# Convolution and SwiGLU block: unit 1 moved from TensorE to a channel-major convolution on the other engines, unit 2 moved to TensorE, with a shorter start

## The chip, the cores and the metric

The kernel runs on one core of a Trainium2 chip. The metric is the device time of one execution in microseconds (us). Times are medians over some executions with their range.

In this program matrix products are on TensorE (PE); VectorE (DVE), ScalarE (ACT) and GpSimd (POOL) do elementwise work. GpSimd also starts the loads that cast float32 to float16, and SyncE (SP) starts nearly all other transfers, one after the other.

## The reference

A depthwise causal convolution with seven softmax weights a head is followed by a SwiGLU block:

```python
w = softmax(weight)                        # (8 heads, 7 taps)
x_pad = pad 6 zeros ahead of x             # x: (8, 4096, 192)
out[b, s, h, g] = sum_k w[h, k] * x_pad[b, s + k, h, g]     # 24 channels a head
g = out @ w_gate;  v = out @ w_val         # (192, 1536) each
result = (g * sigmoid(g) * v) @ w_out      # (1536, 192), 32768 tokens in all
```

## The kernel before

The 32,768 tokens are 64 blocks of 512, and four blocks are a unit. A block is 12 steps. A step multiplies a block with 128 columns of the gate and of the value weights (three matmul pairs each), ACT makes the SiLU, DVE the product, and the down projection follows some steps later. So step n belongs to block n // 12 and unit n // 48.

There are three ways to convolve. Unit 0 has a special early path. Units 1 and 3 are done on TensorE by banded matmuls, in two halves of 32 matmuls placed between steps. All others ("pooled") are done with channels on partitions:

```python
POOLED = (2, *range(4, NU))                 # NU = 16 units

def cast_x(u):      # POOL: one casting load of a unit's input, DRAM to DRAM scratch, ~770 KB
    xs[u] = dpool.tile([rows, D], fp16, tag="xs", name="xs")
    seq(nc.gpsimd.dma_start(out=..., in_=...))          # [cut]

def turn_x(u, i, at):   # SyncE: scratch to SBUF, transposed; needs the whole cast
    seq(nc.sync.dma_start_transpose(out=t, in_=rows[:, at : at + P]))

def place(u, i):        # SyncE: four copies that build the two shared channel tiles of a block
    t0, t1, t2 = xc[b]
    y = y2[u, i // 2][Q * (i % 2) : Q * (i % 2) + Q, :]
    for dst, src in (
        (t1[0:Q, 0:TB], t0[Q:P, 0:TB]), (t1[Q:P, 0:TB], y),
        (t2[0:Q, 0:TB], y),             (t2[Q:P, 0:TB], t0[0:Q, 0:TB]),
    ):
        seq(nc.sync.dma_start(out=dst, in_=src))
```

A pooled unit has six jobs: four of kind "block" (128 of the 192 channels of a block) and two of kind "pair" (the remaining 64 channels of two blocks). In a job ACT makes two or three of the seven taps, DVE two, which it adds itself, and POOL the others and the remaining sums. A block can be placed when its own job and its pair's job are done. The program decides at which step each transfer enters SyncE's order:

```python
def planned(v):                             # steps at which the transfers of unit v are queued
    ...
    if v == 2:   cast, jobs = 21, 55;  times = (36, 36, 36, 38, 39, 39, 41, 41, 43, 43)
    elif v == 3: cast, jobs = 60, 56;  times = range(66, 86, 2)         # [not used: 3 is on TensorE]
    else:        cast, jobs = s0 - 115, s0 - 89;  times = range(s0 - 105, s0 - 85, 2)   # s0 = 48 v

done = max(finished[job] for job in need)   # program step at which POOL's part is queued
if n < max(done + (12 if u == 2 else 18), ustep * u + NCH * i - 16):
    break
place(u, i)
```

## Time and profile before

| | before |
|---|---|
| median of 3 runs | 779.17 us (777.87 to 779.5) |
| span of the profiled run | 776.0 us |
| TensorE busy | 767.9 us, 99% |
| clock granted to TensorE | full from 3.67 us to the last matmuls |
| first gate matmul | 8.43 us |
| plain block of 12 steps | 11.73 us |
| gate matmuls waiting for copies `pxc<-pxc`, `pxc<-y` | none |

`xs<-in_x_dram` is the casting load of a pooled unit, `x<-xs` a transpose out of it (or, as a plain copy `x<-x` of 66 KB, the join of two halves), `pxc<-pxc` and `pxc<-y` the copies of `place`, `x<-x` in a pair of 480 KB the `dup_x` of a TensorE unit, `scr<-tm` the writes of a TensorE unit's result to scratch. A gate matmul `gate<-pxc` needs what POOL wrote itself and, from the second of its three pairs on, what `place` copied.

### The profile page before, as it was taken

What the parts mean: (1) busy time and instruction counts of PE and PEld (TensorE: products, weight loads), DVE (VectorE), ACT (ScalarE), POOL (GpSimd) and SP (SyncE); (2) the same over time, 40 slices, a digit from 0 to 9 for tenths busy, and PEclk for the clock granted to TensorE, in tenths of its full rate; (3) what the DMA queues carried; (4) which work ended last, traced back from release to release, by engine and by line L of the source; (5) the groups of instructions that cost most, each with busy time, mean ns of one, the idle gap of its engine ahead of it and who ended that gap; (6) DMA issues with size and microseconds to landing.
All of it is one profiled execution on the core that took longest, in us unless ns stands there. A gap on an engine that the chain in (4) does not pass through costs nothing.

```text
span 776.0 us, 27834 instructions
## 1 busy us (share of the span) xinstructions
PE 767.9 (99%) x11179; PEld 599.6 (77%) x11179; DVE 687.4 (89%) x1034; ACT 607.6 (78%) x1067; POOL 597.8 (77%) x551
## 2 busy tenths in 40 slices
PE   8999999999999999999999999999999999999997
PEld 5666666668888888888888888888888888887876
DVE  7687998999999999999999999999999999997775
ACT  6576887888878878878888888888888788776664
POOL 9100697799999999999999999999999999992000
PEclk9999999999999999999999999999999999999999
DMA  9949854754534536255353443535445352221211
GB/s 136 186 117 125 170 127 102 166 102 102 114 95 104 103 94 124 65 118 118 84 112 86 103 111 77 115 88 116 93 105 115 77 122 70 70 66 38 70 57 42
DMA packets 143651, 79.31 MB, mean 102 GB/s; under 512 B 89146, under 2 KB 143042, under 8 KB 143042
## 3 DMA queue, kind: packets, MB, share of 16 engines
q1 hardware_dynamic: 130690, 61.58, 34.8%
q0 software_dynamic: 12832, 15.96, 13.5%
q8 instruction: 87, 1.43, 0.8%
q14 instruction: 42, 0.34, 0.1%
HBM read 31.92 MB, written 37.83 MB: 90 GB/s over the span
## 4 chain that ended last, share of the span: by engine, by line
PE 97%; POOL 1%; DMA 1%; DVE 1%; issue 0%; ACT 0%; DVEq 0%; POOLq 0%
PE val L777 41%; PE acc L803 33%; PE gate L777 22%; DMA xe<-in_x_dram 1%; POOL w L168 0%; DVE h L788 0%; POOL xe L98 0%; PE cv L476 0%; PE acc L824 0%; PE cv L387 0%; PE turn L445 0%; ACT sig L786 0%; DVE o_sb L862 0%; ACT o_sb L970 0%; POOL jn L192 0%
## 5 line engine op out<-in xcount | busy, mean ns | idle before, releaser
L786 ACT ACTIVATE sig<-gate 128x512 f16<-128x512 f32 x768 | 448.9, 599 | 154.6 <-PE gate L777 105.3
L788 DVE TENSOR_TENSOR h<-sig,val 128x512 f16<-128x512 f16 x768 | 495.2, 683 | 79.4 <-PE gate L777 45.9
L777 PEld LDWEIGHTS <-w 64*128 64x128 f16 x4608 | 338.9, 110 | 135.2 <-issue 1.9
L777 PE MATMUL gate<-pxc,w 64*128 64x512 f16 x1872 | 438.7, 376 | 0.0
L777 PE MATMUL val<-pxc,w 64*128 64x512 f16 x1872 | 437.6, 376 | 0.5
L803 PE MATMUL acc<-wo,h 64*128 64x192 f16 x6096 | 329.7, 243 | 0.8 <-issue 0.7
L803 PEld LDWEIGHTS <-h 64*128 64x128 f16 x6096 | 300.6, 94 | 28.2 <-ACT sig L786 2.1
L632 POOL TENSOR_TENSOR total<-total,part 128x512 f32<-128x512 f32 x130 | 173.0, 1330 | 45.6 <-DVE total L657 21.8
L657 DVE SCALAR_TENSOR_TENSOR total<-x,both_taps,total 128x512 f32<-128x512 f16 x156 | 166.3, 1066 | 0.0
L647 POOL TENSOR_SCALAR piece<-x,both_taps 128x512 f32<-128x512 f16 x182 | 154.4, 848 | 0.0
L632 POOL TENSOR_TENSOR total<-total,piece 128x512 f32<-128x512 f32 x104 | 141.6, 1362 | 8.7
L777 PE MATMUL gate<-xc,w 64*128 64x512 f16 x432 | 102.1, 377 | 0.0
L777 PE MATMUL val<-xc,w 64*128 64x512 f16 x432 | 101.9, 376 | 0.1
L682 ACT ACTIVATE part<-x,both_taps 128x512 f32<-128x512 f16 x130 | 93.3, 718 | 0.0
L632 POOL TENSOR_TENSOR pxc<-total,piece 128x512 f16<-128x512 f32 x52 | 70.3, 1353 | 4.3
L682 ACT ACTIVATE total<-x,both_taps 128x512 f32<-128x512 f16 x78 | 55.7, 714 | 0.0
L632 POOL TENSOR_TENSOR y<-total,piece 128x512 f16<-128x512 f32 x26 | 33.1, 1273 | 2.2
L862 DVE COPY o_sb<-acc 128x384 f32<-128x384 f32 x63 | 34.5, 547 | 0.0
L861 ACT COPY o_sb<-acc 128x384 f32<-128x384 f32 x63 | 29.6, 471 | 0.1
L98 POOL DMA_DIRECT2D x<-in_x_dram x6 | 5.1, 870 | 24.4 <-ACT sig L786 24.4
L504 POOL COPY tm<-tm 128x1280 f16<-128x1280 f16 x2 | 2.5, 1249 | 19.5 <-DVE tm L493 19.5
L590 POOL DMA_DIRECT2D xs<-in_x_dram x13 | 7.2, 555 | 0.0
(67 smaller groups left out, 74.1 us busy)
## 6 DMA issues: line engine op xcount, KB each, us to landing
out_dram<-o_sb SPq DMA_DIRECT2D x63, 384.0 KB
pxc<-pxc SPq DMA_DIRECT2D x104, 64.0 KB
pxc<-y SPq DMA_DIRECT2D x104, 64.0 KB
xs<-in_x_dram POOLq DMA_DIRECT2D x7, 768.0 KB, 6.7
xs<-in_x_dram POOLq DMA_DIRECT2D x6, 774.0 KB, 6.7
x<-in_x_dram POOLq DMA_DIRECT2D x6, 480.0 KB, 9.4
scr<-tm SPq DMA_DIRECT2D x14, 130.0 KB
x<-x SPq DMA_DIRECT2D x26, 66.0 KB
```

What stands on the lines that cost most here:

```text
L98: nc.gpsimd.dma_start(out=t[p0 + i0 : p0 + i1, w0 - at : w1 - at, :], in_=bass.AP(tensor=x_flat.tensor, offset=(t0 + size * w0 - pad + i0) ...
L590: nc.gpsimd.dma_start(out=flat[skip * D : rows * D].rearrange("(a n) -> a n", n=n), in_=bass.AP(tensor=x_flat.tensor, offset=(u * UT - XP ...
L632: nc.gpsimd.tensor_tensor(job["dst"] if k == K - 1 else total, total, part, op=ALU.add)
L647: nc.gpsimd.tensor_scalar(part, shifted(k), scalar1=job["tap"][:, k : k + 1], scalar2=1.0, op0=ALU.mult, op1=ALU.mult,)
L657: nc.vector.scalar_tensor_tensor(job["total"], shifted(k), job["tap"][:, k : k + 1], job["total"], op0=ALU.mult, op1=ALU.add,)
L682: nc.scalar.activation(part, shifted(k), AF.Copy, scale=job["tap"][:, k : k + 1])
L777: nc.tensor.matmul(o, w16[m][p0 : p0 + Q, k, e::E], xc[b][k][p0 : p0 + Q, 0:TB], start=(k == 0), stop=(k == SL - 1),)
L786: silu[n] = seq(nc.scalar.activation(sg, g, AF.Silu)).ins
L788: seq(nc.vector.tensor_tensor(hj, sg, v, op=ALU.mult))
L803: nc.tensor.matmul(acc[b][bank][:, s, :], hj[p0 : p0 + Q, ts(2 * bank + s, P)], wo16[p0 : p0 + Q, j, :], start=(not second and j == 0 and ...
L861: seq(nc.scalar.copy(o_sb[:, 0:2, :], acc[b][0]))
L862: seq(nc.vector.tensor_copy(o_sb[:, 2:4, :], acc[b][1]))
```

## The change

The intent is to take one of two convolved units off TensorE, the busiest engine. Unit 1 becomes pooled, which fills the time in which POOL, DVE and ACT have room; unit 2 takes the TensorE path in its place, and unit 3 is pooled like the later ones. The start is trimmed as well: fewer fillers before the tap matmuls, the band built by halves of the heads, the value weights in one transfer a third.

```diff
-    POOLED = (2, *range(4, NU))
+    POOLED = (1, *range(3, NU))
 [load_w: value weights in one transfer a third, not two, so a step reads its weight slices in rotated order; iota behind it]
-    x16_tile(1)                      # unit 1's four loads for TensorE
-    for r in range(2):
-        for low in (0, 32):
-            load_x(1, r, low=low)
 [tap matmuls and band by halves of the heads, each half in one PSUM bank]
-        if v == 2:
-            cast, jobs = 21, 55
-            times = (36, 36, 36, 38, 39, 39, 41, 41, 43, 43)
-        elif v == 3:
-            cast, jobs = 60, 56
-            times = range(66, 86, 2)
+        if v == 1:
+            jobs = 19
+            times = (13, 13, 14, 15, 16, 24, 25, 26, 28, 30)
         else:
-            cast, jobs = s0 - 115, s0 - 89
+            jobs = s0 - 89
             times = range(s0 - 105, s0 - 85, 2)
-        plan.setdefault(cast, []).append(lambda: cast_x(v))
+            plan.setdefault(s0 - 115, []).append(lambda: cast_x(v))
 [taps also at steps 20, 23 and 26]
-            if n < max(done + (12 if u == 2 else 18), ustep * u + NCH * i - 16):
+            if n < max(done + (9 if u == 1 else 18), ustep * u + NCH * i - 16):
-    keep_warm(8)
+    keep_warm(6)
+    keep_warm(1, P)
     spread_taps()
-    keep_warm(4, 2 * P)
+    keep_warm(5, 2 * P)
 [...]
+    cast_x(1)
-        at = (25, 31) if u == 0 else (10, 22)     # steps of the convolution halves
+        at = (10, 22)
```

More of the change, by code (lines that the diff above doesn't have):

```diff
@@ L127, in x16_tile, with load_x @@
         x16[u] = cpool.tile([P, 4 * NG, D], fp16, tag="x16", name="x16")
-    def load_x(u, r, after=None, low=0):
-        t, t0, w0, p0 = x16[u], u * UT, 4 * NG * r, Q * r + low
+    def load_x(u, r, after=None):
+        t, t0, w0, p0 = x16[u], u * UT, 4 * NG * r, Q * r
         w1 = w0 + 4 * NG
@@ L161, in load_w @@
         f0, f1 = WF * m, WF * m + WF
-        for half, src, i0, i1, s0 in (
-            (0, moe_w_gate, 0, SL, 0),
-            (1, moe_w_val, 0, SL - 1, 1),
-            (1, moe_w_val, SL - 1, SL, 0),
-        ):
+        for half, src in enumerate((moe_w_gate, moe_w_val)):
             seq(
                 nc.gpsimd.dma_start(
-                    out=w16[m][Q * half : Q * half + Q, i0:i1, :],
-                    in_=src[Q * s0 : Q * (s0 + i1 - i0), f0:f1].rearrange(
-                        "(s q) f -> q s f", q=Q
-                    ),
+                    out=w16[m][Q * half : Q * half + Q],
+                    in_=src[:, f0:f1].rearrange("(s q) f -> q s f", q=Q),
                 )
@@ L195 @@
     xe_load(0)
+    load_w(0)
     cid = small("cid", [P, P], i32)
     seq(nc.gpsimd.iota(cid, pattern=[[1, P]], base=0, channel_multiplier=0))
-    load_w(0)
     load_w(1)
@@ L328, in make_wide @@
         ]
-        for n in range(4):
-            c0 = 16 * 2 * H * (n % 2)
-            seq(
-                nc.tensor.matmul(
-                    banks[n // 2][:, c0 : c0 + 16 * 2 * H],
-                    shift[:, n].rearrange("p r i -> p (r i)"),
-                    spread.rearrange("p j a h -> p (j a h)"),
-                    start=(n % 2 == 0),
-                    stop=True,
-                    skip_group_check=True,
-                )
-            )
-        seq(nc.vector.tensor_copy(pf, pid))
-        for h0 in (0, 4):
+        half = H // 2
+        for hh in range(2):
+            for n in range(4):
+                c0 = 16 * H * n
+                seq(
+                    nc.tensor.matmul(
+                        banks[hh][:, c0 : c0 + 16 * H],
+                        shift[:, n].rearrange("p r i -> p (r i)"),
+                        spread[:, :, :, half * hh : half * hh + half].rearrange(
+                            "p j a h -> p (j a) h"
+                        ),
+                        start=(n == 0),
+                        stop=True,
+                        skip_group_check=True,
+                    )
+                )
+        for hh in range(2):
             for n in range(2):
@@ L345, in make_wide @@
                     (nc.scalar.copy, nc.vector.tensor_copy)[n](
-                        wide[:, :, h0 : h0 + 4, 32 * n : 32 * n + 32],
-                        banks[n].rearrange("p (j a h) -> p a h j", a=2, h=H)[
-                            :, :, h0 : h0 + 4, :
-                        ],
+                        wide[:, :, half * hh : half * hh + half, 32 * n : 32 * n + 32],
+                        banks[hh][:, 32 * H * n : 32 * H * n + 32 * H].rearrange(
+                            "p (j a h) -> p a h j", a=2, h=half
+                        ),
                     )
                 )
+        seq(nc.vector.tensor_copy(pf, pid))
         seq(
@@ L746, in pooled_work @@
         step_now[0] = n
-        if not busy and j != 4:
+        if not busy and (j in (1, 7, 10) or n in (20, 23, 26)):
             ready = dve_steps[0][0] if dve_steps else None
             ahead = act_steps[0][0] if act_steps else n_jobs[0]
-            if j in (1, 7, 10) and ready is not None:
+            if ready is not None:
                 dve_steps.pop(0)[1]()
-            if j in (1, 7, 10) and act_steps and (ready is None or ahead < ready + 3):
+            if act_steps and (ready is None or ahead < ready + 3):
                 act_steps.pop(0)[1]()
@@ L778, in gate_val @@
                         o,
-                        w16[m][p0 : p0 + Q, k, e::E],
+                        w16[m][p0 : p0 + Q, (k + half) % SL, e::E],
                         xc[b][k][p0 : p0 + Q, 0:TB],
@@ L932 @@
             efetch(3)
-        if n == 34:
+        if n == 10:
             make_picks()
-        if n == 37:
+        if n == 13:
             make_channel_taps()
@@ L946 @@
                     conv_out(u + 1, m)
-            lo = 32 if u == 0 else 28
-            if ls in range(lo, lo + 12, 3):
-                fetch(UB * (u + 1) + (ls - lo) // 3)
+            if ls in range(28, 40, 3):
+                fetch(UB * (u + 1) + (ls - 28) // 3)
         if u + 2 < NU and not pooled(u + 2):
```

## The prediction

> **What bounds the kernel now.** I read the page's busy shares first, then the slices, the chain that ended last, the windows by block, and last the early chain in order of time.
>
> ```profile
> PE 767.9 (99%) x11179; PEld 599.6 (77%) x11179; DVE 687.4 (89%) x1034; ACT 607.6 (78%) x1067; POOL 597.8 (77%) x551
> ...
> POOL 9100697799999999999999999999999999992000
> PEclk9999999999999999999999999999999999999999
> ...
> PE 97%; POOL 1%; DMA 1%; DVE 1%; issue 0%; ACT 0%; DVEq 0%; POOLq 0%
> ```
>
> TensorE is busy 99% of the span at full clock, and 97% of the chain is TensorE. POOL is nearly full from slice 6 (about 100 us) to slice 36 (about 700 us), but idle in slices 3 and 4 (about 40 to 75 us): there is room for POOL work early and none in the middle.
>
> The program makes 64 blocks of 12 steps. A block's start is that of its first gate matmul in the trace: 8.43, 20.34, 37.59, 50.85, 62.89 us and so on. Windows on those starts (columns: length; busy us and count of PE, PEld, DVE, ACT, POOL; clock; DMA share; GB/s):
>
> ```profile
> 8.43:20.34 11.91, 11.62 (x177) 6.99 (x177) 8.57 (x15) 8.07 (x15) 11.01 (x20) 1.00 1.29 180
> 20.34:37.59 17.25, 16.36 (x350) 11.56 (x347) 11.34 (x20) 9.78 (x19) 2.04 (x5) 1.00 1.43 199
> 37.59:50.85 13.26, 13.26 (x237) 9.01 (x233) 11.04 (x19) 9.58 (x17) 1.25 (x1) 1.00 0.41 99
> 62.89:74.62 11.73, 11.73 (x170) 8.00 (x168) 8.38 (x13) 8.15 (x14) 1.71 (x2) 1.00 1.21 134
> 86.35:98.08 11.73, 11.73 (x170) 8.00 (x168) 11.26 (x16) 9.65 (x17) 11.32 (x11) 1.00 0.88 207
> 109.81:122.18 12.37, 12.37 (x202) 8.29 (x200) 11.89 (x18) 10.07 (x18) 11.82 (x11) 1.00 0.49 105
> ```
>
> A plain block takes 11.73 us, also with DVE at 11.26 and POOL at 11.32 of it. The block at 109.81 has 32 more matmuls, half a unit's convolution on TensorE, and takes 12.37: **0.64 us a half**. So whatever is on TensorE counts at full price, and what the other engines do costs nothing while they keep up. 64 x 11.73 = 750.7 of the 776.0 us; the other 25 us are the start, extra TensorE work in the first blocks, the tail, and a few bubbles.
>
> The early chain (columns: start us, us, what):
>
> ```profile
> 1.42 2.17 POOL xe L98 x3
> ...
> 3.84 3.43 POOL w L168 x6
> ...
> 7.87 6.29 DMA xe<-in_x_dram
> 14.21 0.72 PE cv L387 x59
> ...
> 35.96 0.72 issue
> 39.60 0.59 PE cv L476 x32
> ```
>
> The first 14 us are ruled by POOL issuing loads and by the second input load, which lands at 14.16 us. At 35.96 TensorE loses 0.72 us to "issue": it waits for no semaphore.
>
> [...] the chain here shows steps of 0.21 us per gate and val pair, [...] the eight 512-wide fillers run 0.43 us apart until 4.2 us and the 256-wide ones after that 0.11 us apart, [...] here every cast load has a POOL issue of 0.55 to 0.87 us. [...]
>
> **The change, part by part.**
>
> 1. *One unit fewer on TensorE.* Of 16 units, before convolves 1 and 3 on TensorE, after only 2 (unit 0 is early work in both).
>
> ```profile
> L476 PE MATMUL cv<-x,band 64*32 64x240 f16 x128 | 2.6, 266 | 0.0
> L493 DVE CAST tm<-cv 128x480 f16<-128x480 f32 x8 | 4.9, 650 | 0.1
> L493 ACT CAST tm<-cv 128x480 f16<-128x480 f32 x8 | 4.1, 562 | 2.1 <-PE cv L476 2.1
> ```
>
> 128 matmuls become 64, in two halves of 32: 2 x 0.64 = **-1.28 us**, straight off the path. The compiled order confirms it: 60 matmuls fewer (-64, +4 for the halved taps). The four DVE and four ACT evictions of the unit (2.6 and 2.2 us) go too, beside the path.
>
> 2. *Unit 1 goes to ACT, DVE and POOL*: 6 jobs more, 84 for 78.
>
> ```profile
> L632 POOL TENSOR_TENSOR total<-total,part 128x512 f32<-128x512 f32 x130 | 173.0, 1330 | 45.6 <-DVE total L657 21.8 <-ACT sig L786 19.6
> L657 DVE SCALAR_TENSOR_TENSOR total<-x,both_taps,total 128x512 f32<-128x512 f16 x156 | 166.3, 1066 | 0.0
> L647 POOL TENSOR_SCALAR piece<-x,both_taps 128x512 f32<-128x512 f16 x182 | 154.4, 848 | 0.0
> L682 ACT ACTIVATE part<-x,both_taps 128x512 f32<-128x512 f16 x130 | 93.3, 718 | 0.0
> ```
>
> POOL's five convolution groups sum to 572 us over 78 jobs, 7.3 us each, so +44 us on POOL; DVE +12 x 1.07 = 13 us; ACT +16 x 0.72 = 11 us. All of it lies between steps 20 and 75, where POOL had 2.04 and 1.25 us of work in two blocks. Off the path: **0**, if the tiles arrive in time. I followed the program's rule for placing them: unit 1's blocks are copied into place at steps 40, 46, 64 and 76 and needed at 48, 60, 72 and 84; the slack is 8 steps at the least, where unit 2 before had 11. In time: the first two jobs have their last DVE part at step 31, about 45 us, POOL then ends near 53, the copies land near 57, and step 48 comes near 61. For the last block POOL ends near 91, SyncE is then busy with unit 2's nine writes to scratch (they took 6 us for unit 1 before), so the copies may land at 94 to 96 and step 84 comes at 96.5. That margin is about 1 us, and I charge **+0.2 us** for it. From unit 4 on jobs run only 3 steps later than before and are still placed 16 steps ahead: no change.
>
> 3. *Start.* Two fewer fillers and taps by half: the tap matmuls come about 0.4 us earlier and the first copies need one bank only. But the first input load lands at 5.79 and the band is used at 6.08, so at most 0.3 us of this is real; then the first gate weights (landed 8.21) and value weights (8.84 and 9.13) bind. The value weights now are one transfer of 192 KB, which I put at 9.0: the first step gains nothing. One POOL issue fewer per third (0.57 us each) and the iota behind them: DMA engines are by then 1.29 full in the mean, so landing, not issue, rules; I put the second input load 0.3 us earlier. **-0.3 us**, where early work waits for it at step 6.
>
> 4. *Traffic.* Four loads of 480 KB, issued from 16.9 us and landing at 24 to 33 us, are gone; one cast to scratch (landed at 36.4 for unit 2) takes their place and should land near 24. Eight transposes through SyncE (1.25 us each) follow; the first convolution on ACT comes at step 20, near 33 us, so 5 us later than its tile. The 0.72 us of "issue" fell just as the old burst drained. It has an even chance to vanish: **-0.35 us**.
>
> Sum: -1.28 - 0.3 - 0.35 + 0.2 = -1.7; 779.17 - 1.7 = **777.4 us**.
>
> **The rivals.** *A late unit 1.* [...] if the cast lands after 33 us the SiLU behind the first tap waits and TensorE with it; the same if a copy into place is late. For it: margins of 8 steps, and a landing of 36.4 us for the comparable cast before. Against: that one was issued at 21.98 us behind four large loads; now it goes out near 17.5. Cost if it happens: 1 to 4 us, so 778 to 781. *POOL becomes the bound*, since it already is full from 100 to 700 us. Against: the new work lies before that, and placement keeps 16 steps of slack; else 14 units x 44 = 616 us must fit in about 680. I give it little; it would show as several us at unit starts. *The start pays more*: if all of the earlier issue reaches the path and the "issue" gap goes, the gain is 1.28 + 1.0 + 0.7 = 3 us, 776.2. *The conv removed is hidden anyway*: TensorE's extra 0.64 us in the block at 109.81 is measured, so no.
>
> **Range and chances.** The before runs spread over 1.6 us, and bubbles of 0.03 to 0.32 us in the middle blocks sum to some 1.8 us that can come or go. With the rivals: 775.5 to 779.2. 2% is 15.6 us: nothing above comes near it, in either direction. Within 2%: 0.98; 0.01 each side.
>
> **What would show it.** Step 1: 64 convolution matmuls, and one pair of 12.37 us blocks left, moved to units' steps 58 and 70. Step 2: blocks 4 to 7 at 11.73 us apart from those 0.64 us, with POOL full from about 37 us; wrong if a gate matmul at steps 48, 72 or 84 waits for a DMA into the placed tiles, or if ACT's first tap waits for a transpose. Step 3: the first gate matmul within 0.3 us of 8.43 and early work after step 6 before 14.0. Step 4: no "issue" piece of over 0.5 us in the first 45 us. The whole is wrong if the time falls under 775.5 or rises over 779.2.

## More of the kernel before

A unit for TensorE needs its input four times shifted in SBUF; half of this is loaded and the other half comes from `dup_x`, two plain SyncE copies of 480 KB, each partition's row in one piece. (Unit 1 of this kernel loads all four itself, so here only unit 3 has a `dup_x`.)

The page's line of the gate matmuls that read placed tiles (busy us, mean ns, then the idle time before them):

```profile
L777 PE MATMUL gate<-pxc,w 64*128 64x512 f16 x1872 | 438.7, 376 | 0.0
```

## The result, and the profile after

| | before | changed |
|---|---|---|
| median, same session | 778.98 us (777.87 to 779.5, 4 runs) | 786.09 us (783.45 to 787.37, 4 runs) |
| span of the profiled run | 776.0 us | 784.6 us |
| TensorE busy | 767.9 us | 771.4 us |
| mean clock | 0.999 | 0.993 |

The ratio is 1.0089, with a 95% interval of 1.006 to 1.0117. A ratio here is the mean time of one kernel's fast runs over the mean of the other's fast runs of the same rounds, so it isn't quite the ratio of the medians quoted. The change made the kernel 7 us slower. That is still "within 2%", but it is far outside the predicted range of 775.5 to 779.2.

The page of the changed kernel, in the parts that answer to those shown of before: busy times, the clock by slices, the shares of the chain that ended last, and the group of gate matmuls that read placed tiles.

```profile
PE 771.4 (98%) x11119; PEld 579.2 (74%) x11119; DVE 696.0 (89%) x1042; ACT 612.7 (78%) x1079; POOL 633.2 (81%) x584
...
PEclk9998999999999999999999999999999999999999
...
PE 96%; DMA 1%; DVE 1%; ACT 0%; issue 0%; POOL 0%; SPq 0%; DVEq 0%; POOLq 0%
...
L768 PE MATMUL gate<-pxc,w 64*128 64x512 f16 x2016 | 474.9, 378 | 6.5 <-DMA pxc<-pxc 6.2
```

TensorE has 60 matmuls fewer and yet is busy for 3.5 us longer. The clock of the fourth slice (59 to 78 us) has an 8 where before there were only nines. The gate matmuls that read placed tiles, which never waited before, now wait 6.5 us. So there are two things to explain: waiting, and matmuls that run slower.

The windows by block (columns as in the prediction), for the blocks at 61.11, 80.47, 92.84 and 104.57 us (blocks 4 to 7, unit 1's own):

```profile
61.11:80.47 19.36, 15.86 (x204) 12.84 (x202) 12.61 (x18) 10.07 (x18) 11.96 (x12) 0.82 0.59 126
80.47:92.84 12.37, 12.37 (x203) 8.24 (x201) 11.14 (x18) 10.07 (x18) 7.97 (x8) 1.00 0.26 67
92.84:104.57 11.73, 11.73 (x171) 7.98 (x169) 10.28 (x17) 9.66 (x17) 7.38 (x8) 1.00 0.83 157
104.57:121.83 17.26, 14.11 (x170) 9.83 (x168) 11.03 (x16) 9.66 (x17) 10.86 (x11) 0.90 0.50 110
```

Block 4 holds half of unit 2's convolution, so it should take 12.37 us like block 5. It takes 19.36: of the 6.99 too many, 3.50 are idle (19.36 - 15.86) and 3.49 are more busy time for the same matmuls (15.86 - 12.37, clock 0.82). Block 7 should take 11.73 and takes 17.26: 3.15 idle and 2.38 more busy time (clock 0.90). These are **12.5 us in two places**. The timeline and clock records give the order of events: an idle time of 3.50 us ended at 65.16 and the clock was at half for 6.83 us from 64.36; one of 2.66 us ended at 107.61 and the clock was at half for 3.41 us from 108.73. TensorE was busy for 6.02 and 3.30 us of the two half-clock stretches. In the first, gate matmuls started 0.43 us apart (66.15, 66.58, 67.01), against 0.21 ahead of the wait (60.90, 61.11); if, at this pace, half of the busy time is lost, the clock accounts for about 4.7 of the 5.87 us of additional busy time (an estimate from these records). The other 1.2 us need not be the clock's: in `dup_later` below, block 4 is busy 1.05 us longer than 12.37 at a whole clock.

The rest together gained, by the sum over all block starts. Half-units on TensorE: -1.28. The middle blocks from 13 on: -1.76, since their bubbles of before are gone. Block 3: -0.32, likewise. Block 1: -0.60, the "issue" gap with it. Block 2, besides its part of the -1.28: +0.38. The start up to block 1: +0.04. Together -3.5, and +12.5 - 3.5 is the 9.0 us by which the last matmul ends later (771.65 before, 780.66 after).

**The first wait, at step 48.** SyncE's part of the timeline (columns: start us, length us, queue and line, operation, tiles, count):

```profile
47.98 0.47 SPq L603 DMA_DIRECT2D x<-x  x1
...
50.14 2.72 SPq L148 DMA_DIRECT2D x<-x  x2
57.14 1.16 SPq L599 DMA_TRANSPOSE x<-xs  x1
58.40 0.54 SPq L856 DMA_DIRECT2D out_dram<-o_sb  x1
58.99 0.50 SPq L700 DMA_DIRECT2D pxc<-pxc  x1
59.59 1.23 SPq L700 DMA_DIRECT2D pxc<-y  x2
```

and two of POOL's entries in the same stretch:

```profile
47.38 0.54 POOL L584 DMA_DIRECT2D xs<-in_x_dram  x1
...
54.14 1.27 POOL L626 TENSOR_TENSOR y<-total,piece 128x512 f16<-128x512 f32 x1
```

The second of these is the last POOL work that block 4 needs; it ends at 55.4 us, against the 53 of the prediction and with 5.7 us to go to step 48. But SyncE had queued two 480 KB copies for unit 2 at 50.14 and then stood until 57.14 at a transpose for unit 3. That transpose waits for unit 3's casting load, issued at 47.38 right behind POOL's first job, whose pieces of 24,768 bytes held all 16 DMA engines from about 51.5 to 55.5 us, the last of them landing at 57.1. Only at 58.99, behind the issue of a 384 KB output write, did SyncE reach the copies for block 4. The chain in order of time says how long they took:

```profile
58.99 6.14 DMA pxc<-pxc
65.16 0.58 PE gate L768
```

6.14 us for 64 KB. In the transfer records the two 480 KB copies, held up by the cast, occupy the engines from 56 to 62 us, on the same queue ahead of it. Then a transpose and the output write (`out_dram<-o_sb`, its 768-byte pieces started from 62.2 to 64.3 us) run, also ahead of it, and the copies' own 1024-byte pieces start only at 64.2. So the 480 KB copies are the larger part of these 6 us, not all of it.

**The second wait, at step 84.** POOL, then SyncE:

```profile
95.78 1.66 POOL L626 TENSOR_TENSOR pxc<-total,piece 128x512 f16<-128x512 f32 x1
97.39 0.58 POOL L584 DMA_DIRECT2D xs<-in_x_dram  x1
```

```profile
92.70 5.81 SPq L506 DMA_DIRECT2D scr<-tm  x8
...
100.11 5.09 SPq L700 DMA_DIRECT2D pxc<-pxc  x1
105.25 2.05 SPq L700 DMA_DIRECT2D pxc<-y  x2
```

POOL finished the last input of block 7 at 97.44 us and at once issued unit 4's casting load. SyncE was behind nine writes of unit 2's result. (In the kernel before, the same cast went out at 98.30 us, with unit 2's first copies going out at 96.12 for step 96 at 109.81.) When it came to the copies, the issue of the first took 5.09 us instead of the usual 0.5: the cast's pieces held every engine from 99.5 to about 103.5 us, and in the records almost no piece of SyncE's queue ran in that time. An output write issued at 99.19 us was caught too, and ran mostly ahead of the copies, until about 107 us.

So the theory was: *transfers for later units, put by their formulas at these steps, stand ahead of unit 1's copies, in SyncE's order and on the DMA engines.* Rivals: POOL is simply too late with unit 1; the changed start is the culprit; the large pieces of the cast, not its place, are what blocks; the clock, not the wait, is what can be mended.

### The profile page after: what moved, and what is told of

Same layout as the page of the kernel before. It is cut to its first block, busy times and chain, and to the rows that moved or that the text cites.

```text
span 784.6 us, 27800 instructions
## 1 busy us (share of the span) xinstructions
PE 771.4 (98%) x11119; PEld 579.2 (74%) x11119; DVE 696.0 (89%) x1042; ACT 612.7 (78%) x1079; POOL 633.2 (81%) x584
## 3 DMA queue, kind: packets, MB, share of 16 engines
q8 instruction: 87, 1.43, 0.7%
## 4 chain that ended last, share of the span: by engine, by line
PE 96%; DMA 1%; DVE 1%; ACT 0%; issue 0%; POOL 0%; SPq 0%; DVEq 0%; POOLq 0%
PE val L768 51%; PE acc L794 33%; PE gate L768 11%; DMA pxc<-pxc 1%; PE warm L869 1%; PE cv L381 0%; DVE h L779 0%; PE turn L439 0%; POOL total L626 0%; PE acc L815 0%; DMA pxc<-y 0%; SPq L700 0%; ACT sig L777 0%; DVE total L651 0%; PE cv L470 0%
## 5 line engine op out<-in xcount | busy, mean ns | idle before, releaser
L768 PE MATMUL gate<-pxc,w 64*128 64x512 f16 x2016 | 474.9, 378 | 6.5 <-DMA pxc<-pxc 6.2
L768 PE MATMUL val<-pxc,w 64*128 64x512 f16 x2016 | 474.6, 378 | 0.2
L768 PEld LDWEIGHTS <-w 64*128 64x128 f16 x4608 | 324.1, 110 | 169.2 <-issue 11.0
L794 PE MATMUL acc<-wo,h 64*128 64x192 f16 x6096 | 341.7, 243 | 0.0
L794 PEld LDWEIGHTS <-h 64*128 64x128 f16 x6096 | 310.1, 94 | 24.4 <-ACT sig L777 0.9
L651 DVE SCALAR_TENSOR_TENSOR total<-x,both_taps,total 128x512 f32<-128x512 f16 x168 | 178.8, 1064 | 0.0
L626 POOL TENSOR_TENSOR total<-total,piece 128x512 f32<-128x512 f32 x112 | 158.1, 1411 | 9.3
L768 PE MATMUL val<-xc,w 64*128 64x512 f16 x288 | 68.8, 377 | 0.4 <-DVE h L779 0.4
L768 PE MATMUL gate<-xc,w 64*128 64x512 f16 x288 | 68.7, 377 | 0.0
L626 POOL TENSOR_TENSOR y<-total,piece 128x512 f16<-128x512 f32 x28 | 43.2, 1541 | 2.3
```

The source lines that it names most:

```text
L626: nc.gpsimd.tensor_tensor(job["dst"] if k == K - 1 else total, total, part, op=ALU.add)
L651: nc.vector.scalar_tensor_tensor(job["total"], shifted(k), job["tap"][:, k : k + 1], job["total"], op0=ALU.mult, op1=ALU.add,)
L768: nc.tensor.matmul(o, w16[m][p0 : p0 + Q, (k + half) % SL, e::E], xc[b][k][p0 : p0 + Q, 0:TB], start=(k == 0), stop=(k == SL - 1),)
L794: nc.tensor.matmul(acc[b][bank][:, s, :], hj[p0 : p0 + Q, ts(2 * bank + s, P)], wo16[p0 : p0 + Q, j, :], start=(not second and j == 0 and ...
```

## The experiments

All gave correct results. The edits are to the changed kernel unless said. The before kernel's median in the same session is in parentheses.

**Earlier casts.** The casting loads are moved in time, one at a time and both.

```diff
+            cast = s0 - 115                      # unit 3: 29, unit 4: 77
+            if v == 3: cast = 17                 # cast3_early, behind the SiLU of step 16
+            if v == 4: cast = 54                 # cast4_early;  both in both_casts_early
-            plan.setdefault(s0 - 115, []).append(lambda: cast_x(v))
+            plan.setdefault(cast, []).append(lambda: cast_x(v))
```

Expected of cast3_early:

> Only the cast of unit 3 to scratch goes out earlier (behind the SiLU of step 16 in place of step 29, where it ran from 51.4 to 57.1 us). Theory A (the cast's 24.8 KB descriptors hold all 16 DMA engines and SyncE stands behind it, so the copies into place for block 4 went out 3.6 us after their data and landed 6.1 us after that): the stall at step 48 (block 4 took 19.36 us, 7.63 too many) goes, the one at step 84 (block 7, 17.27 us) stays; 786.1 becomes about 778.5. Theory B (POOL, DVE and ACT make unit 1 too late; the margin of 8 steps is too small): both stalls stay, 786. Theory C (the duplicating copies of unit 2's input, 2 x 480 KB ahead in the same queue, are what delays the copies): block 4 stays over 15 us, about 783.

Measured: 786.96 us (785.76 to 787.93; before 778.03), ratio 1.0108. A miss. Blocks 4 and 7 took 19.13 and 16.84 us, and block 1 took 18.42 where it had taken 16.64. The early cast held back the first unit's scratch reads (37.3 us in the changed kernel, 43.4 here), and SyncE was late in all that followed: the 480 KB copies went out at 58.1, the copies for block 4 at 63.86. Removing one obstacle only shifted the others into the same place.

Expected of cast4_early:

> Only the cast of unit 4 goes out earlier in POOL's order (step 54 in place of 77, so before and not after POOL's last job of unit 1). Theory A: block 7 returns from 17.27 to about 11.7 us and block 4 stays at about 19.4: 786.1 becomes about 780.6. Theory B: block 7 stays over 15 us, 786.

Measured: 781.17 us (778.33 to 781.65; before 778.03), ratio 1.0031. A hit. In SyncE's timeline the first copy for block 7 now is

```profile
99.72 0.47 SPq L700 DMA_DIRECT2D pxc<-pxc  x1
```

0.47 us for the issue that took 5.09, at the same time. Block 7 takes 12.20 us and block 4 still 18.72. So the cast of unit 4 caused nearly all of the second wait, and POOL wasn't too late there.

Expected of both_casts_early:

> Both of the moves above. Theory A: both stalls go; blocks 4 and 7 at 11.7 us, no half-clock stretch after the start, about 773 to 774, so under the kernel before by some 0.7%. Theory B: 786, stalls stay. Theory C: block 7 mended alone, about 780.

Measured: 784.36 us (784.19 to 787.14; before 778.03), ratio 1.0088. A miss by all three theories. Block 4 fell to 13.84 us and block 7 to 12.26, but blocks 3 and 6 now took 16.25 and 14.03: gate matmuls of block 3 waited 2.4 us for the last scratch reads of unit 0, those of block 6 for their copies. The lateness moved on to others.

**The size of the pieces.** The cast is cut to pieces of 1.1 to 1.5 KB in place of 24 KB.

```diff
-        n = (rows - skip) * D // P               # 128 pieces of 24 KB
+        g = 4 if skip else 3
+        n, m = g * D, (rows - skip) // (16 * g)  # 16 x m pieces of g rows
```

> All casts where the change has them, but each cut into descriptors of 1.1 to 1.5 KB in place of 24.8 KB. If it is the size of the descriptors that shuts out the other queue (A1), SyncE's transfers interleave: the copy into place that took 5.1 us to issue and 108.8 us to land goes through in 2 to 3 us and block 7 falls to under 13 us; block 4 improves in part, since SyncE still waits in order for the cast to land before a transpose: about 779 to 782. If it is the bytes alone (A2), the stalls stay within 1 us, 785 to 787.

Measured: 788.51 us (786.78 to 789.73; before 778.03), ratio 1.0131. Blocks 4 and 7 took 20.96 and 16.87 us, and the waits were 4.92 and 2.92 us. SyncE's issue of the first copy for block 7 fell from 5.09 to 0.47 us, but the wait for the copies, 2.92 us, was no shorter than the 2.66 us of the changed kernel. From 101.5 to 103.0 us only pieces of the cast were running, small as they were. So in this run smaller pieces moved the waiting from the issue to behind it and took nothing off it. That is A2 in kind, though the time is 1.5 us above A2's range and block 4 waited 1.4 us longer than in the changed kernel. (The expectation's "108.8 us to land" is the time at which the copies had landed.)

**The order on SyncE.** Either the 480 KB copies or the transposes of unit 3 are moved behind the copies for block 4.

```diff
-            if ls == (37 if u == 0 else 26):
+            if ls == (42 if u == 0 else 26):     # dup_later
                 dup_x(u + 2)
-            times = range(s0 - 105, s0 - 85, 2)
+            if v == 3: times = range(41, 61, 2)  # turn_later (39 to 57 before)
```

> One edit to the changed kernel: unit 2's duplicating copies (2 x 480 KB on SyncE's queue) go out at step 42, behind block 4's copies into place (step 40), and not at 37. All four profiles of the change so far land block 4's copies at 65.0 to 66.6 us, whatever the cast of unit 3 did. Theory C (the duplicates ahead in the same queue): they land at 61 to 63.5 us, the stall at step 48 falls from 3.5 us and a half-clock stretch to 2 us or less and block 4 from 19.4 to about 14: 786.1 becomes 780 to 781.5. Theory A as it was (the cast of unit 3 alone): block 4 stays at 19. Block 7 stays at about 17 in either.

Measured: 783.69 us (781.04 to 785.11; before 777.25), ratio 1.0077. Half a hit: block 4 fell from 19.36 to 15.16 us and its wait to 1.43, after which the clock stayed whole. Block 7, which was to stay at 17, fell to 14.22 too: its cast was where it had been, but this time the first copy's issue took 3.34 us and not 5.09, the wait was 1.64 us, and the clock stayed whole. The middle blocks from 13 on had 2.64 us of small bubbles that the changed kernel doesn't have, so the time fell by less than the two blocks. SyncE's timeline shows what remained:

```profile
45.78 13.66 SPq L599 DMA_TRANSPOSE x<-xs  x2
...
60.16 0.47 SPq L700 DMA_DIRECT2D pxc<-pxc  x1
```

It stood for 13.66 us at two transposes that wait for the cast of unit 3, with the copies for block 4 behind them in order. With the 480 KB copies no longer ahead of them (only two transposes and a 384 KB output write), these then were late by 1.4 us only.

> One edit to the changed kernel: the transposes of unit 3 start at step 41, behind block 4's copies, and not at 39, so that SyncE does not stand before them for the cast of unit 3 (landed 57.1 us). SyncE then issues block 4's copies at 55.5 to 58 us in place of 59 to 62. If the wait in SyncE's order is what counts, block 4 falls to about 13 us and the time to about 780; if the queue behind it is full of the duplicates anyway (theory C), the copies still land after 62.5 us, the stall stays over 1.5 us: 781 to 785.

Measured: 787.27 us (784.91 to 800.35; before 777.25), ratio 1.0117. The 800.35 us are the one slow execution (mean clock 0.983); the three fast ones have a median of 786.2, and the ratio uses them alone. Theory C's signs came, a landing after 62.5 us and a wait of over 1.5; its 781 to 785 us did not. The copies for block 4 are now issued with no transpose of unit 3 waiting ahead of them:

```profile
51.26 3.75 SPq L148 DMA_DIRECT2D x<-x  x2
...
58.44 0.74 SPq L700 DMA_DIRECT2D pxc<-pxc  x1
```

and landed at about 66.3 us all the same, after a wait of 4.6 us, behind the 480 KB copies. So the order of issue alone isn't the cause, nor is the queue alone: with either one mended the other holds the copies.

**All three at once**: dup at 42, transposes of unit 3 from 41, cast of unit 4 at step 54.

> Both of these edits and the early cast of unit 4 (which brought block 7 from 17.27 to 12.2 us). If transfers ahead in SyncE's order and queue are the whole of the loss, no gate matmul waits over 0.5 us after step 20, the clock stays whole, and the time is 773.5 to 775, so some 0.5% under the kernel before. If unit 1 is made too late by the engines themselves (theory B), blocks 4, 6 or 7 keep stalls and it stays over 778.

Measured: 781.36 us (780.2 to 784.15; before 777.25), ratio 1.0063. A miss of the 773.5 to 775 us that order alone was to give. Block 4 took 12.70 us and block 7 12.64: both waits are mended. But block 6 took 17.09:

```profile
70.74 6.87 SPq L599 DMA_TRANSPOSE x<-xs  x2
...
86.30 0.47 SPq L700 DMA_DIRECT2D pxc<-pxc  x1
```

Unit 4's cast, early now, was issued at 70.19 us; SyncE then stood at two transposes of unit 3 from 70.74 to 77.6 us (6.87 us, where three took 3.88 in the changed kernel), and the copies for block 6, ready at 78.1, were issued at 86.30. A wait of 2.68 us followed, and a clock of 0.90.

**The start alone**, on the kernel before (fillers, taps by halves, one value transfer; units as before).

> The kernel before with the start of the change alone (seven fillers, taps by halves of heads, value weights in one transfer, the rotated order of weight slices). The prediction gave this part 0.3 us. The profile of the change had its first gate matmul at 8.89 us and not 8.43, with the clock whole only from 6.33 us and not 3.67; four other profiles of kernels with this start have 8.27 to 8.63. So: between 0.3 us faster and 0.3 us slower than the kernel before, ratio 0.9990 to 1.0005, with the first gate matmul at 8.2 to 8.9.

Measured over 5 rounds: 777.72 us (776.81 to 778.57; before 777.25), ratio 1.0004, interval 0.9991 to 1.0016. The start part of the change is worth nothing measurable either way, so it causes neither the loss nor a gain. In this profile the first gate matmul came at 8.90 us; the clock became whole at 6.35 us, where before it was 3.67. Over the profiles of all kernels here this onset lay between 3.67 and 6.35, whatever the start.

**Transfers in the gaps.** All are set between the copies of unit 1, none right ahead of them, and unit 4's cast comes after those of block 7.

```diff
-            if ls == (37 if u == 0 else 26):
+            if ls == (42 if u == 0 else 26):
+            if v == 3: times = (47, 48, 49, 54, 55, 65, 66, 67, 77, 78)
+            if v == 4: cast, times = 81, range(91, 111, 2)
```

> The changed kernel with SyncE's and POOL's order arranged around block 4 to 7's copies into place: the duplicates of unit 2 at step 42; unit 3's transposes at steps 47 to 78, in the gaps between the copies, and not at 39 to 57; unit 4's cast back at step 81 with its transposes from 91. In the last try (duplicates, transposes and cast of unit 4 moved) block 4 was mended (19.36 to 12.70, of which 0.64 is unit 2's convolution) but block 6 lost 5.4 us: its copies, whose data was ready at 78.1 us, went out at 86.3, behind unit 3's transposes. If order alone is the loss, no gate matmul waits over 0.5 us after step 20, and the time is 773.5 to 775, 0.5% under the kernel before. If another block takes the stall over, 777 to 782.

Measured over 5 rounds: **775.79 us** (775.42 to 775.89; before 779.05), ratio 0.9956, interval 0.9943 to 0.997. It beats both kernels, with the clock whole from 6.18 us to the last matmuls, and lies just above the expected 773.5 to 775 us. Blocks 4 to 7 took 12.74, 12.37, 11.73 and 13.66 us, against 19.36, 12.37, 11.73 and 17.27. GpSimd was done with block 4 at 55.3 us, as in the changed kernel (55.4), so it wasn't too late there either. One wait of this kind is left in the list of waits, and SyncE's timeline has its reason:

```profile
PE gate L772 <- DMA pxc<-pxc: 1.4, 1, 1.4
```

```profile
88.62 5.17 SPq L506 DMA_DIRECT2D scr<-tm  x8
...
95.28 0.47 SPq L700 DMA_DIRECT2D pxc<-pxc  x1
```

GpSimd was done with block 7 at 90.69 us, but the nine writes of unit 2 stood ahead of its copies.

**The clock.** Fillers into the two waits were to keep TensorE active while it waits.

```diff
         m, e = divmod(j, E)
+        for _ in range({48: 15, 84: 12}.get(n, 0)):
+            [one 512-wide matmul on a constant, into the gate bank]
```

> The changed kernel with 15 and 12 filler matmuls (0.22 us each) put ahead of the first gate matmul of steps 48 and 84, where TensorE waits 3.5 and 2.7 us for a copy. If part of each stall is the half clock that follows the idle stretch (6.83 and 3.41 us at half clock in the profile, some 3.2 and 1.7 us lost), the clock stays whole, block 4 falls from 19.4 to about 16.3, block 7 from 17.3 to about 15.6, and 786 becomes 781 to 782.5. If the half clock costs nothing because the data is late anyway, 785 to 787.

Measured: 788.48 us (783.41 to 791.87; before 779.05), ratio 1.0115. A miss. The timeline of TensorE at step 48:

```profile
61.44 3.41 PE L766 MATMUL gate<-fill 128*128 128x512 f16 x15
...
72.32 0.58 PE L775 MATMUL gate<-pxc,w 64*128 64x512 f16 x1 [7.13 <-DMA pxc<-pxc]
```

In this execution, the slowest of the four, the fillers (3.41 us) ended long before the wait did: another 7.13 us were idle, since the second 480 KB copy took until 63.2 us only to be issued, and the clock was at half from 69.91 to 76.74 us after all. At step 84 the fillers did what they were for: 12 of them filled 2.76 us, 0.61 us stayed idle, the clock stayed whole. Blocks 6 and 7 were together 4.47 us too long there; the changed kernel lost 5.54 at this place, and 4.78 in its repetition below. So the wait's length varies more between executions than fillers return, and the experiment doesn't settle the clock's share in the time. (Two executions that weren't profiled kept a mean clock of 0.999 and 1.000 and took 783.41 and 786.27 us, so a whole clock alone doesn't give back the 7 us.) That share rests on the windows and the clock records alone.

**The changed kernel once more**, in the session of the last two.

> The changed kernel unaltered, on this chip beside the two others: 784 to 787.5 us, ratio 1.008 to 1.012, with stalls at steps 48 and 84 of 3 to 4.5 us before the first matmul that needs a copied tile.

Measured: 788.77 us (785.37 to 789.99; before 779.05), ratio 1.0118. Blocks 4 and 7 took 19.53 and 16.51 us, with waits of 4.71 and 2.61 us, so the two waits are there again. The ratio is inside what was expected; the median, and both waits, are a little outside.

**The last wait of the spaced kernel.** One number is changed in it: the copies of block 7 enter SyncE's order at step 70, ahead of the nine writes.

```diff
-            if n < max(done + (9 if u == 1 else 18), ...):
+            lag = 3 if (u, i) == (1, 3) else 9 if u == 1 else 18
+            if n < max(done + lag, ...):
```

> This is the spaced kernel with one number changed: the copies that complete unit 1's last block enter SyncE's order at step 70, ahead of the nine writes of unit 2's convolution to the scratch memory, instead of at step 76 behind them. In the spaced kernel's trace one wait is left: at step 84 a gate matmul waited 1.39 us for those copies; GpSimd had finished their input at 90.69 us, SyncE issued them from 95.28 to 98.88 us behind the writes (88.62 to 94.64 us), and the block took 13.66 us instead of 11.73. Theory A (SyncE's order is all that delays them): they are issued from about 90.8 us, land by 95 us, the block returns to about 11.8 us, and the time falls by 1.5 to 1.9 us to 773.9 to 774.3 us. Theory B (the transfers themselves are late, whatever their place): the wait stays above 1 us and the time is 775.5 to 776 us as before. Theory C (the writes, now behind the copies, delay the transposes of unit 2 or unit 3): a new wait appears in the two blocks after, and the time stays at or above 775.5 us.

Measured over 14 runs: 776.57 us (774.7 to 784.6; before 777.37), ratio 1.0, interval 0.9982 to 1.0017. The copies were issued from 90.53 us and block 7 took 11.73: that wait is gone. In the list of waits there is another:

```profile
PE gate L773 <- DMA xc<-scr: 1.6, 1, 1.6
```

The nine writes, now behind the copies, ended at 98.9 instead of 94.6 us, the scratch reads of unit 2 behind them came late for step 96, and block 8 took 13.50 us. So both the first theory (order alone delays the copies) and the third (the writes then delay something else) held: block 7 gained 1.93 us, block 8 lost 1.77, 0.97 us of small bubbles came back in the middle blocks, and the gain was nil. The runs also scatter over 10 us where the spaced kernel's scattered over 0.5; the two slowest had a mean clock of 0.997, but they weren't profiled, so which wait they met is open. I keep the spaced kernel as the better version, with the caution that it was measured in one session, in 5 runs.

## Why the prediction was wrong

*Step 1, one unit fewer on TensorE, was right.* 128 convolution matmuls became 64, the pair of 0.64 us went from blocks 8 and 9, and unit 2's pair replaced unit 1's: -1.28 us.

*Step 2 failed*, with its sentence "the copies land near 57, and step 48 comes near 61" and its charge of +0.2 us. Step 48 came at 61.11 us, but the first of the copies landed at 65.13; blocks 4 and 7 together took 12.5 us too long. GpSimd's own times were about right: 55.4 against 53, and at block 7 97.4 against 91, which the 7.0 us lost at the first wait account for. ACT's first tap didn't wait for a transpose, so the first half of the rival "a late unit 1" didn't come true; its second half, "the same if a copy into place is late", did. Step 2's "the slack is 8 steps at the least" counted from the step at which the copies enter the program's order. (The rivals did name these margins as a point for a late unit 1, and set against it only that the cast now goes out earlier.) What counts is the time from POOL's last sum to the use, 5.7 us, and in it SyncE had 480 KB copies, transposes and a wait for unit 3's cast to get through. For block 7 I did count SyncE's writes, and found a margin of about 1 us; what I missed was unit 4's cast, which POOL issued at 97.39 us, the moment it was done, and whose pieces then held the DMA engines from 99.5 to about 103.5 us. The statement that nothing changes from unit 4 on looked at jobs and placing, not at when their casts would run.

*The size of that rival was wrong too.* It was put at "1 to 4 us". Measured were 6.65 us of wait in two places, plus 5.87 us of slower matmuls behind it, about 4.7 of them by the clock, as estimated above. The prediction had put no cost of a lower clock behind a wait. In these traces an idle time of 2.66 us was followed by 3.41 us at half clock, and one of 2.68 us, in `dup_turn_cast4`, by a block with a clock of 0.90; after waits of 1.43 and 1.64 us, in `dup_later`, the clock stayed whole. What decides it was not shown.

*Step 3, -0.3 us, is not there*: the start alone gave a ratio of 1.0004, and block 1 of the changed kernel began at 20.38 us, before at 20.34. The first gate matmul was 0.46 us later, not within 0.3.

*Step 4, -0.35 us, was about right in size, by luck*: block 1 became 0.60 shorter and its 0.72 us of "issue" went, but block 2 has a new piece of 0.56 us at 41.92, against my test that none be over 0.5, and lost 0.38. Together -0.22. (The even chance given to the 0.72 us was an estimate; no trace shows what that "issue" is.) The loss in block 2 belongs to step 2 and its charge of 0 for the other engines. A tap of unit 1 on DVE (1.16 us from 41.39) stands right ahead of a product `h` for which TensorE then waits 0.43 us, in every profile with unit 1 pooled and in none with it on TensorE. The chain and the list of waits say:

```profile
41.39 0.53 DVE total L651
41.92 0.56 issue
```

```profile
PE val L768 <- DVE h L779: 0.4, 1, 0.4
```

*One reading was loose*: the 512-wide fillers at the start run 0.43 us apart until 3.53 us, not 4.2; the clock was whole from 3.67, and the next came after 0.29. Nothing rests on it.

*A term that was missing*: I allowed that the 1.8 us of middle bubbles "can come or go", and they went, all of them, as did the 0.32 in block 3. Why isn't tested: `start_only` keeps 1.66 us of them, and four variants with the changed kernel's units have 0.97 to 2.64 us again. Without the two waits the changed kernel would, by this estimate, have been 3.5 us under the profiled execution of before (777.75 us), so near 774.2, outside the range on its other side. The spaced kernel's trace agrees: with 2.3 us of lost time left in blocks 4 and 7, its last matmul ended at 770.30 us, 1.35 earlier than before. That its median is 3.3 us better has a second reason: the profiled execution of before was its fastest, and where its slower ones lose the rest was not profiled.

What is shown: each obstacle by its own experiment (the 480 KB copies by dup_later and turn_later together, unit 3's transposes by the same pair, unit 4's cast by cast4_early), and all of them by the spaced kernel, which mends them by times alone. What is argued only: the share of the clock. What was not tested: what sets the order in which the pieces of the cast and of SyncE's transfers run, and the 384 KB output write that stands right ahead of the copies in the changed kernel and in the spaced one too.

## What to carry to other kernels

When work moves to another unit or engine, list every transfer of *other* units that shares its issuing engine and the DMA engines in the time between "input ready" and "needed", and count that time in microseconds, not in program steps. What stands ahead of a small copy belongs in the count: here 64 KB took 6.14 us from issue to landing behind two copies of 480 KB, a transpose and an output write of 384 KB, and 2.97 us for the last copy of block 7 in the spaced kernel, behind an output write and its sister copies. A slack that the old order had by accident isn't the new order's slack: the times of three transfers for later units follow from formulas that the diff leaves as they were (for unit 3 it only drops an exception), and with what followed from them they cost 12.5 us. Mending one obstacle in a full stretch tends to move the wait to the next user, as four of these experiments show, so plan the whole stretch at once.
